# Attention, a routed MLP and a gated MLP in one kernel: eight ScalarE products issued later in each tile, and the weight ring placed 64 bytes off

## The chip, the cores and the metric

The kernel runs on one core of one Trainium2 chip, as one program. The metric is the device time of that program in microseconds (us). Before the change it is 657.42 us, the median of three runs (657.04 to 659.06).

## The reference, cut to what matters

```python
# 1. recurrent attention, B=4, H=8, S=768, D=48
for t in range(S):
    cur = u * kt (outer) vt
    y[t] = rt . (state + cur)
    state = w * state + kt (outer) vt
# 2. a routed MLP on x = y as (3072, 384): 8 experts, 384 -> 1024 -> 384
do_compute = x @ w_skip > 0
e = argmax(x @ w_gate); g = softmax at e
out = x + g * relu(x @ w1[e]) @ w2[e]    # only where do_compute
# 3. a gated MLP
out = (((x @ w1) * (x @ w2)) @ w3) @ w_out
```

The term with `u` (each token's own key and value, the bonus) needs no state: for each token and head it is one number, z = sum over d of r*u*k, times the vector v.

## The kernel before, in words

**Attention (0 to about 178 us).** The 3072 tokens are cut into 24 tiles of 128 (two batches of 64 tokens each), and a loop over n = 0 to 21 is software-pipelined by hand; two last tiles follow it, written out. Each engine runs its instructions in the order in which the loop emits them. In iteration n:

- VectorE makes FK of tile n+2 (`prep`, L359, two SBUF tensors multiplied), scales the state S (`state_copy`, L407, in two iterations of four), evacuates the masked scores Fs of tile n+1 (`evac`, L371), reduces z of tile n+1 (`bonus`, L389), and later adds the bonus to the result of tile n: xg (`x_out`, L440).
- TensorE makes the scores sc of tile n+1 (L366), the result y of tile n (`y_mm`, L419 and L422) in one of two PSUM banks, called y and G in turn, the router's logits of tile n-1 (L464, into a corner of the same bank), three transposes T of tile n-1 (`x_trans`, L451), and the new state (`ds_mm`, L435). Between them `keep` puts matmuls of W = w3 @ w_out (L711, bank wp), a product that the third part needs, or filling matmuls (L255) where its inputs are not there.
- ScalarE copies the state to SBUF (Ss, L409), takes a step of narrowing the 64-bit weights (L103), makes the bonus products zv of tile n+1 (`prep_v`, L399: one ACTIVATE for each of 8 heads, v times z), copies the turned x out of bank T (xT, L453), the logits L (L467) and, where a block of W is done, its high half W_hi (L683). VectorE takes the low half W_lo behind it (L691).
- GpSimd multiplies m (L384, L385: the r*u*k that z sums) and kd (L378).

Tiles are routed in groups of 6, 6, 4, 4 and 4. When a group is full, `route_a` (VectorE) finds the expert of each token, and `route_b` in the next iteration counts by matmul (L507, L509, L510, into a corner of bank G or y); ScalarE copies the counts out (r_pr, L516). The next logits go into the same bank as the counts, and wait for that copy. `run_todo`, called in the middle and at the end of an iteration, issues the steps that are due. The middle of an iteration before the change:

```python
w_step(WN[n][0])
prep_v(n + 1)
w_ready()
y_mm(n)
keep(4 * WK[n][0])
run_todo()
if n > 0:
    x_trans(n - 1)
keep(4 * WK[n][1])
w_step(WN[n][1])
w_evac(0)
x_out(n)
ds_mm(n)
```

**Experts (about 200 to 347 us).** Each of 64 weight pieces (raw, from DRAM, buffers `stg`) is split by ScalarE into ehi (L84) and by VectorE into elo (L85) in a ring of ten pairs: three in pool `ring0`, allocated from the upper end of SBUF beside `stg0`, seven in `ring1`. TensorE reads ehi and elo as stationary operand in L929 and as moving operand in L948. All of this is fp32 in two parts.

**Gated MLP (to the end).** Six blocks of 512 tokens: matmuls L1129 and L1149.

SBUF pools are stacked, so a tile's address follows from the sizes of those before it. Before the change the ring, and everything stacked above or below it, begins at a multiple of 128 bytes.

Of the kernel before, what the change touches and what calls it, by code (L numbers as in the profile page):

```python
# [8 lines left out]
F32 = mybir.dt.float32  # L9
# [9 lines left out]
P = 128  # L19
# [38 lines left out]
def fused_kernel(ctx, tc, att, kv, wt, u, wg, we, w3, wo, w12, r, k, v, wu, out):  # L58
# [18 lines left out]
    E(tc.tile_pool(name="edge", bufs=1, side="right")).tile([P, 24], F32, name="edge")  # L77
    stg = [E(tc.tile_pool(name="stg0", bufs=2, side="right")), None]
    rctx = ExitStack()
    rings = [rctx.enter_context(tc.tile_pool(name="ring0", bufs=RG, side="right")), None]  # L80
    yctx = ExitStack()

# [110 lines left out]
    def load_expert(e, q):  # L193
        raw = stg[(4 * e + q) % 3 // 2].tile([P, 2, 2 * D], F32, name="raw")
        nc.sync.dma_start(out=raw, in_=we[e, :, 2 * q:2 * q + 2, :])
        return raw
# [29 lines left out]
    with tc.manual_schedule():  # L226
# [10 lines left out]
        def load_t(n):  # L237
            nc.sync.dma_start(out=TB[n % 3].rearrange("p a h t -> p (a h t)"), in_=att[n])
# [51 lines left out]
        for i in range(6):  # L290
            wn = pw[:, i - 1] if i else wc
            n = 1 << i
# [62 lines left out]
        def prep(n):  # L355

            t = TB[n % 3]
            FK = FK_[n] = wk.tile([P, 2, NH, CH], F32, name="FK", bufs=3)
            nc.vector.tensor_tensor(out=FK, in0=t, in1=UT[:, n // 2 % 2], op=ALU.mult)  # L359

        def scores(n):
            FK = FK_[n]
            sc = ps_1.tile([P, 512], F32, tag="sc", name="sc").rearrange("p (h t) -> p h t", h=NH)
            for h in range(NH):
                for m, d in zip(half, dims):
                    nc.tensor.matmul(sc[m, h], FK[d, 1, h], FK[d, 0, h], start=True, stop=True)  # L366
            return sc

        def evac(n, sc):
            Fs = Fs_[n] = wk.tile([P, NH, CH], F32, name="Fs")  # L370
            nc.vector.tensor_tensor(out=Fs, in0=sc, in1=mask[:, None, :].to_broadcast([P, NH, CH]), op=ALU.mult)  # L371

        def prep_k(n):

            c, bp = divmod(n, 2)
            if c < NC - 1:
                kd = kd_[n] = wk.tile([P, NH, HD], F32, name="kd")
                nc.gpsimd.tensor_tensor(out=kd, in0=KV[bp][c % 2][:, 1], in1=KU[:, c % 2], op=ALU.mult)  # L378

        def prep_m(n):  # L380

            c, bp = divmod(n, 2)
            m = P_[n] = wk.tile([P, NH, HD], F32, name="m")
            nc.gpsimd.tensor_tensor(out=m, in0=KV[bp][c % 2][:, 0], in1=un, op=ALU.mult)  # L384
            nc.gpsimd.tensor_tensor(out=m, in0=KV[bp][c % 2][:, 1], in1=m, op=ALU.mult)  # L385

        def bonus(n):
            z = z_[n] = wk.tile([P, 32], F32, name="z")[:, 0:NH]
            nc.vector.tensor_reduce(out=z, in_=P_.pop(n), axis=AX.X, op=ALU.add)  # L389

        def prep_v(n, eng=None):
            c, bp = divmod(n, 2)
            v, z = KV[bp][c % 2][:, 2], z_.pop(n)
            zv = zv_[n] = wk.tile([P, NH, HD], F32, name="zv")
            if eng:
                eng.tensor_tensor(out=zv, in0=v, in1=z[:, :, None].to_broadcast([P, NH, HD]), op=ALU.mult)
            else:
                for h in range(NH):
                    nc.scalar.activation(out=zv[:, h], in_=v[:, h], func=AF.Copy, scale=z[:, h:h + 1])  # L399

        def state_copy(n):
            c, bp = divmod(n, 2)
            s = S[bp]
            if c == 0:
                return
            if c % 2 == 0:
                nc.vector.tensor_tensor(out=s, in0=s, in1=w128[:, :, None].to_broadcast([P, NH, HD]),  # L407
                                        op=ALU.mult)
            nc.scalar.copy(out=Ss[bp], in_=s)  # L409

        def y_mm(n, tag="y"):

            c, bp = divmod(n, 2)
            v, Fs, FK = KV[bp][c % 2][:, 2], Fs_.pop(n), FK_.pop(n)
            y = G if n % 2 and n < NT - 2 else ps_1.tile([P, 512], F32, tag=tag, name="y")
            yv = y[:, 0:D].rearrange("p (h d) -> p h d", h=NH)
            for h in range(NH):
                for m in half:
                    nc.tensor.matmul(yv[m, h], Fs[m, h], v[m, h], start=(h == 0), stop=True, skip_group_check=True)  # L419
            for h in range(NH if c else 0):  # L420
                for m, d in zip(half, dims):
                    nc.tensor.matmul(yv[m, h], FK[d, 0, h], Ss[bp][d, h], start=False, stop=True,  # L422
                                     skip_group_check=True)
            y_[n] = y
            if n < NT - 2:
                yb[0] = y
# [19 lines left out]
        def x_trans(n, bank=None):  # L446
            xg = x_.pop(n)
            xb_[n] = T if bank is None else bank
            pT = xb_[n][:, 0:D].rearrange("p (k t) -> p k t", k=ND)
            for k in range(ND):  # L450
                nc.tensor.transpose(pT[:, k], xg[:, P * k:P * k + P], ident)  # L451
            xT_[n] = wk.tile([P, ND, P], F32, name="xT", bufs=2)
            nc.scalar.copy(out=xT_[n], in_=pT)  # L453
# [137 lines left out]
        def place_mm(bp=0):  # L591
            for o, oh, v in pend:
                nc.tensor.matmul(SL[bp][:, o], oh, v, start=False, stop=True, skip_group_check=True)
            pend.clear()
# [78 lines left out]
        def w_step(k):  # L673
            for _ in range(k):
                next(wprep, None)
# [3 lines left out]
        def w_evac(k):  # L679

            while k < len(w_out):
                f, ps = w_out[k]
                nc.scalar.copy(out=W_hi[:, f], in_=ps)  # L683
                w_out[k:k + 1] = []
                w_lo.append((f, ps))
# [8 lines left out]
        def w_ready():  # L694
            done.update(fresh[0])
            fresh[:] = [fresh[1], []]
# [22 lines left out]
        def idle_mm():  # L719
            if spare[0] is None and (w_out or w_lo):  # L720
                w_evac(0)
                w_evac2()
            dummy(DQ)
            dummy(DQ)

        def keep(k):

            due[0] += k
            while due[0] > 0:
                if next(wmm, None):  # L730
                    due[0] -= 4
                else:
                    idle_mm()
                    due[0] -= 2
# [28 lines left out]
        def run_todo(late=False):  # L763
            now, todo[:] = todo[:], []
            for fn, args in now:
                if late and fn is route_b:
                    todo.append((fn, args))
                    continue
                fn(*args)
                if fn is logits_out:  # L770
                    if args[0] in last_of:
                        todo.append((route_a, (last_of[args[0]],)))
                elif fn in NEXT:
                    todo.append((NEXT[fn], args))

        for n in range(NT - 2):
            w_ready()
            if n == NT - 3:
                raws = {q: load_expert(0, q) for q in range(2)}
            if n + 4 < NT:  # L780
                load_t(n + 4)
            prep(n + 2)
            state_copy(n + 1)
            sc = scores(n + 1)
            prep_k(n + 1)
            prep_m(n + 2)
            evac(n + 1, sc)
            bonus(n + 1)
            if n == NT - 3:
                bonus(NT - 1)  # L790
            next(more_consts, None)
            w_step(WN[n][0])
            prep_v(n + 1)
            w_ready()
            y_mm(n)
            keep(4 * WK[n][0])
            run_todo()
            if n > 0:
                x_trans(n - 1)
            keep(4 * WK[n][1])  # L800
            w_step(WN[n][1])
            w_evac(0)
            x_out(n)
            ds_mm(n)
            place_mm(n % 2)
            if n + 4 < NT:
                load_v(n + 4)
            if n < NT - 3:
                place(3)
            w_step(WN[n][2])  # L810
            run_todo(n < NT - 3)
            if n > 0:
                todo.append((logits, (n - 1,)))
            w_evac2()
# [41 lines left out]
    M = mctx.enter_context  # L856
# [40 lines left out]
        w_evac2()  # L897
    wctx.close()
    stg[1] = M(tc.tile_pool(name="stg1", bufs=1, reuse_waits="tile"))
    rings[1] = M(tc.tile_pool(name="ring1", bufs=NRING - RG, reuse_waits="tile"))  # L900
    nr2 = M(tc.tile_pool(name="nr2", bufs=1, reuse_waits="tile"))

# [463 lines left out]
```

## Time and profile before

| | us |
|---|---|
| median of 3 runs | 657.42 |
| the profiled execution | 658.01 |
| its span, first to last instruction | 656.2 |
| TensorE matmul busy | 625.2 (95%) |
| VectorE busy | 364.1 (55%) |
| ScalarE busy | 255.5 (39%) |
| GpSimd busy | 140.3 (21%) |
| mean granted TensorE clock | 0.984 |

Busy shares are over the whole span. The three parts have different limits, so the engine that matters is read stage by stage: which wait ends last there. In the timeline a row is start, duration, engine, line, operation, output<-inputs, shapes and count; brackets give the engine's idle time before it and what ended it.

### The profile page before, as it was taken

The numbers are of one execution on the slowest core, as the hardware profiler recorded it, in microseconds if no ns is written. First come the engines' busy times: TensorE is split into PE (matmuls) and PEld (weight loads), VectorE is DVE, ScalarE is ACT, GpSimd is POOL, SyncE is SP. The second block draws the span as 40 slices with busy tenths as digits, with TensorE's granted clock in tenths as the row PEclk, the third lists the DMA queues.
The fourth block names the chain that finished last, engine by engine and source line by source line (L and its number), as shares of the span: only waits on it lengthen the run. The fifth ranks groups of instructions, "written<-read, shape, count | busy, mean of one in ns | idle before, by whom it ended". The sixth has DMA issues, their size and how long they took to land.

```text
span 656.2 us, 14005 instructions
## 1 busy us (share of the span) xinstructions
PE 625.2 (95%) x5866; PEld 537.9 (82%) x5866; DVE 364.1 (55%) x641; ACT 255.5 (39%) x592; POOL 140.3 (21%) x134
## 2 busy tenths in 40 slices
PE   7979599997998999999999999999999999999996
PEld 6868487886767999999997888888888888888884
DVE  6699897997567889899874321321330330331320
ACT  2556454343325556666643222222221231221220
POOL 4887365543122123223122000000000000000000
PEclk9899899997999999999999999999999999999998
DMA  8889778554427878877522002002002002001001
GB/s 312 339 284 374 257 263 292 191 161 131 137 79 261 269 253 258 297 283 259 186 68 67 0 17 80 1 17 80 1 16 81 1 16 81 0 1 49 0 2 52
DMA packets 26791, 90.53 MB, mean 138 GB/s; under 512 B 4009, under 2 KB 10298, under 8 KB 25696
## 3 DMA queue, kind: packets, MB, share of 16 engines
q1 hardware_dynamic: 24672, 84.11, 37.1%
q0 software_dynamic: 2048, 5.44, 2.3%
q8 instruction: 48, 0.79, 0.5%
q14 instruction: 23, 0.19, 0.1%
HBM read 77.81 MB, written 12.58 MB: 138 GB/s over the span
## 4 chain that ended last, share of the span: by engine, by line
PE 76%; DVE 9%; issue 5%; DMA 4%; ACT 2%; POOL 1%; SPq 0%; ACTq 0%; DVEq 0%; POOLq 0%
PE ab L1129 30%; PE po L1149 15%; PE hp L929 8%; PE y L948 8%; PE wp L711 4%; DMA TB<-in_att 2%; PE sc L366 2%; DVE FK L359 1%; PE S L435 1%; ACT zv L399 1%; PE G L464 1%; DMA KV<-in_kv 1%; PE y L422 1%; PE y L419 1%; PE pT L1109 1%
## 5 line engine op out<-in xcount | busy, mean ns | idle before, releaser
L1136 DVE TENSOR_TENSOR p_sb<-ab,a_sb 128x512 f32<-128x512 f32 x48 | 33.2, 692 | 155.6 <-PE ab L1129 155.6
L1129 PE MATMUL ab<-bxh,w12h 128*128 128x512 f32 x288 | 112.4, 390 | 0.6 <-ACT bxh L1168 0.6
L1129 PE MATMUL ab<-bxh,w12l 128*128 128x512 f32 x288 | 112.1, 389 | 0.0
L1129 PE MATMUL ab<-bxl,w12h 128*128 128x512 f32 x288 | 112.0, 390 | 0.0
L1137 ACT CAST ph<-p_sb 128x512 fp32r<-128x512 f32 x48 | 29.8, 622 | 106.4 <-DVE p_sb L1136 106.4
L85 DVE TENSOR_TENSOR elo<-raw,ehi 128x768 fp32r<-128x768 f32 x64 | 60.8, 956 | 8.7 <-ACT ehi L84 8.3
L1129 PEld LDWEIGHTS ab<-bxh,w12h 128*128 128x128 f32 x288 | 54.1, 188 | 12.6 <-ACT bxh L1168 1.5
L1129 PEld LDWEIGHTS ab<-bxl,w12h 128*128 128x128 f32 x288 | 54.0, 188 | 11.7 <-DVE bxl L1170 0.4
L1129 PEld LDWEIGHTS ab<-bxh,w12l 128*128 128x128 f32 x288 | 54.1, 188 | 11.2
L399 ACT ACTIVATE zv<-KV,z 128x48 f32<-128x48 f32 x184 | 44.0, 324 | 34.1 <-issue 17.8
L1149 PE MATMUL po<-ph,W_hi 128*128 128x512 f32 x144 | 57.0, 396 | 0.0
L1149 PE MATMUL po<-pl,W_hi 128*128 128x512 f32 x144 | 56.1, 390 | 0.0
L929 PE MATMUL hp<-xh,ehi 128*128 128x256 f32 x192 | 54.9, 287 | 1.3 <-ACT xh L880 0.9
L1149 PE MATMUL po<-ph,W_lo 128*128 128x512 f32 x144 | 56.0, 389 | 0.0
L711 PE MATMUL wp<-wo_s,w 128*128 128x384 f32 x128 | 52.8, 525 | 3.3 <-DVE w L118 2.2
L84 ACT CAST ehi<-raw 128x768 fp32r<-128x768 f32 x64 | 52.7, 829 | 2.9 <-DMA raw<-in_we 2.9
L929 PE MATMUL hp<-xh,elo 128*128 128x256 f32 x192 | 53.8, 282 | 0.0
L929 PE MATMUL hp<-xl,ehi 128*128 128x256 f32 x192 | 53.7, 282 | 0.0
L1138 DVE TENSOR_TENSOR pl<-p_sb,ph 128x512 fp32r<-128x512 f32 x48 | 33.3, 693 | 33.0 <-ACT ph L1137 33.0
L932 ACT ACTIVATE hh<-hp 128x256 fp32r<-128x256 f32 x64 | 24.7, 386 | 49.4 <-PE hp L929 47.6
L948 PE MATMUL y<-ehi,hh 128*128 128x384 f32 x128 | 43.3, 338 | 0.0
L948 PE MATMUL y<-elo,hh 128*128 128x384 f32 x128 | 43.2, 338 | 0.0
(207 smaller groups left out, 1174.7 us busy)
## 6 DMA issues: line engine op xcount, KB each, us to landing
raw<-in_we SPq DMA_DIRECT2D x32, 768.0 KB, 5.6
KV<-in_kv SPq DMA_DIRECT2D x24, 576.0 KB, 5.1
TB<-in_att SPq DMA_DIRECT2D x24, 512.0 KB, 8.0
raww<-in_w SPq DMA_DIRECT2D x8, 1024.0 KB, 8.5
raw<-in_w SPq DMA_DIRECT2D x8, 768.0 KB, 7.4
xm<-xg SPq DMA_DIRECT2D x48, 96.0 KB, 2.2
out<-ob SPq DMA_DIRECT2D x18, 256.0 KB, 2.0
x<-xm SPq DMA_DIRECT2D x20, 192.0 KB, 2.5
```

Of the source, the lines that this page charges most:

```text
L84: nc.scalar.copy(out=hi, in_=raw)
L85: (eng or nc.vector).tensor_tensor(out=lo, in0=raw, in1=hi.bitcast(F32), op=ALU.subtract)
L399: nc.scalar.activation(out=zv[:, h], in_=v[:, h], func=AF.Copy, scale=z[:, h:h + 1])
L711: nc.tensor.matmul(ps, w3[:, g], wo_s[:, g], start=(g == 0), stop=(g == NF - 1))
L929: nc.tensor.matmul(hp, a, b, start=(i == 0), stop=(i == 8))
L932: nc.scalar.activation(out=hh, in_=hp, func=AF.Relu)
L948: nc.tensor.matmul(ys[e, t], a[:, P * t:P * t + P], b[:, D:2 * D], start=(f == 0 and i == 0), stop=(f == NF - 1 and i == 2))
L1129: nc.tensor.matmul(q, a, b, start=(i == 0), stop=(i == 8))
L1136: nc.vector.tensor_tensor(out=p_sb, in0=ps[1], in1=a_sb, op=ALU.mult)
L1137: nc.scalar.copy(out=ph, in_=p_sb)
L1138: nc.vector.tensor_tensor(out=pl, in0=p_sb, in1=ph.bitcast(F32), op=ALU.subtract)
L1149: nc.tensor.matmul(po, a[:, f, c], b, start=(i == 0), stop=(i == 3 * NF - 1))
```

## The change

`prep_v(n + 1)` is emitted later in the iteration: behind the first `run_todo()` (which issues the counts' copy) and behind `x_trans(n - 1)` (which issues the copy of turned x). It is still ahead of `w_evac(0)`, `x_out(n)` and the second `run_todo` with the logits' copy. Two unused tiles of 64 bytes are allocated, one between `stg0` and `ring0`, one between `stg1` and `ring1`. So the ring, and what is stacked beyond it (the buffers of the narrowed weights, the gathered tokens xr, raw2), begin 64 bytes past a multiple of 128; `stg` (raw) stays at a multiple of 128.

```diff
     stg = [E(tc.tile_pool(name="stg0", bufs=2, side="right")), None]
     rctx = ExitStack()
+    rctx.enter_context(tc.tile_pool(name="edge0", bufs=1, side="right")).tile([P, 16], F32, name="edge0")
     rings = [rctx.enter_context(tc.tile_pool(name="ring0", bufs=RG, side="right")), None]
...
             w_step(WN[n][0])
-            prep_v(n + 1)
             w_ready()
             y_mm(n)
             keep(4 * WK[n][0])
             run_todo()
             if n > 0:
                 x_trans(n - 1)
+            prep_v(n + 1)
             keep(4 * WK[n][1])
...
     stg[1] = M(tc.tile_pool(name="stg1", bufs=1, reuse_waits="tile"))
+    M(tc.tile_pool(name="edge1", bufs=1, reuse_waits="tile")).tile([P, 16], F32, name="edge1")
     rings[1] = M(tc.tile_pool(name="ring1", bufs=NRING - RG, reuse_waits="tile"))
```

No engine gets or loses an instruction, and the orders of TensorE, VectorE, GpSimd and the DMA queues stay as they were. Only ScalarE's order changes. Around the counts of the first group, before (zv is the product of `prep_v`, W_hi<-wp the copy of a block of W, r_d the router's exponential, r_pr the counts):

```order
L399 ACTIVATE zv<-KV_0_110,z 128x48 x8
L683 CAST W_hi<-wp_118 128x384
L494 ACTIVATE r_d_1243<-r_d_1243 128x48
L453 COPY xT<-T 128x384
L103 ACTIVATE w_1287<-raww 128x1024
L467 COPY L<-y 128x9
L409 COPY Ss_112<-S_191 128x384
L399 ACTIVATE zv<-KV_1_109,z 128x48 x8
L516 COPY r_pr<-G 128x48
L453 COPY xT<-T 128x384
L467 COPY L<-G 128x9
```

and ScalarE at the same place in the changed kernel, whose lines stand one lower:

```order
L684 CAST W_hi<-wp_122 128x384
L495 ACTIVATE r_d_1238<-r_d_1238 128x48
L454 COPY xT<-T 128x384
L400 ACTIVATE zv<-KV_0_114,z 128x48 x8
L104 ACTIVATE w_1291<-raww 128x1024
L468 COPY L<-y 128x9
L410 COPY Ss_116<-S_195 128x384
L517 COPY r_pr<-G 128x48
L454 COPY xT<-T 128x384
L400 ACTIVATE zv<-KV_1_113,z 128x48 x8
L468 COPY L<-G 128x9
```

W_hi and r_d now stand ahead of one zv, and r_pr ahead of the next; w, L and Ss stand behind the first. One block of W later, on ScalarE, around the counts of the second group, before:

```order
L399 ACTIVATE zv<-KV_1_111,z 128x48 x8
L494 ACTIVATE r_d_1959<-r_d_1959 128x48
L453 COPY xT<-T 128x384
L683 CAST W_hi<-wp_118 128x384
L103 ACTIVATE w_2002<-raww 128x1024
L467 COPY L<-y 128x9
L409 COPY Ss_112<-S_191 128x384
L399 ACTIVATE zv<-KV_0_108,z 128x48 x8
L516 COPY r_pr<-G 128x48
```

and ScalarE there in the changed kernel:

```order
L495 ACTIVATE r_d_1954<-r_d_1954 128x48
L454 COPY xT<-T 128x384
L400 ACTIVATE zv<-KV_1_115,z 128x48 x8
L684 CAST W_hi<-wp_122 128x384
L104 ACTIVATE w_2006<-raww 128x1024
L468 COPY L<-y 128x9
L410 COPY Ss_116<-S_195 128x384
L517 COPY r_pr<-G 128x48
```

Here zv moves between xT and W_hi: W_hi, with VectorE's W_lo waiting for it, keeps its place behind zv, but zv now stands behind the transposes' copy. The third counts (16 tiles in) combine both: r_pr moves ahead of zv, and the W_hi that follows stays behind it.

## Rows read from the trace of the kernel before

**Rows 1.** The page, part 2: TensorE's busy tenths in 40 slices of 16.4 us.

```profile
PE   7979599997998999999999999999999999999996
```

**Rows 2.** Waits of TensorE, 0 to 200 us: total us, times, longest.

```profile
PE G L464 <- ACT r_pr L516: 10.2, 3, 6.0
```

**Rows 3.** Timeline, 66 to 84 us: counts of the first group.

```profile
69.62 0.56 DVE L691 TENSOR_TENSOR W_lo<-wp,W_hi 128x384 fp32r<-128x384 f32 x1 [0.90 <-ACT W_hi L683]
...
70.80 0.24 ACT L494 ACTIVATE r_d<-r_d 128x48 f32<-128x48 f32 x1 [1.22 <-DVE r_oh L493]
...
72.41 0.49 ACT L409 COPY Ss<-S 128x384 f32<-128x384 f32 x1
...
76.23 1.91 ACT L399 ACTIVATE zv<-KV,z 128x48 f32<-128x48 f32 x8 [3.33 <-issue]
...
78.04 0.18 ACT L516 COPY r_pr<-G 128x48 f32<-128x48 f32 x1
...
78.27 1.45 PE L464 MATMUL G<-wgs,xT 128*128 128x9 f32 x6 [5.96 <-ACT r_pr L516]
...
83.46 1.11 PE L366 MATMUL sc<-FK 48*64 48x64 f32 x32
```

**Rows 4.** Timeline of TensorE, 20 to 50 us: an earlier stall.

```profile
39.07 0.91 PE L711 MATMUL wp<-wo_s,w 128*128 128x384 f32 x2 [2.18 <-DVE w L118]
```

**Rows 5.** Windows: busy us of PE, PEld, DVE, ACT, POOL; clock; DMA share, GB/s.

```profile
78.20:82.70 4.50, 4.43 (x13) 2.99 (x13) 2.75 (x9) 0.57 (x3) 0.00 (x0) 0.53 0.21 56
```

**Rows 6.** Waits of VectorE, 79 to 111 us.

```profile
DVE xg L440 <- PE G L464: 2.0, 1, 2.0
DVE xg L440 <- ACT zv L399: 1.5, 1, 1.5
DVE xg L440 <- PE y L464: 1.4, 2, 0.8
DVE Fs L371 <- PE sc L366: 1.0, 1, 1.0
```

**Rows 7.** Timeline, 117 to 127 us: a block of W, counts of the second group.

```profile
117.32 0.48 ACT L453 COPY xT<-T 128x384 f32<-128x384 f32 x1 [0.70 <-PE T L451]
...
118.21 0.56 DVE L691 TENSOR_TENSOR W_lo<-wp,W_hi 128x384 fp32r<-128x384 f32 x1
...
123.65 0.84 PE L464 MATMUL G<-wgs,xT 128*128 128x9 f32 x6 [0.47 <-ACT r_pr L516]
...
124.58 0.56 DVE L440 TENSOR_TENSOR xg<-G,zv 128x384 f32<-128x384 f32 x1 [0.82 <-issue]
...
124.96 0.48 ACT L453 COPY xT<-T 128x384 f32<-128x384 f32 x1 [1.36 <-PE T L451]
...
126.84 1.11 PE L366 MATMUL sc<-FK 48*64 48x64 f32 x32
```

**Rows 8.** Timeline, 152 to 162 us: counts of the third group.

```profile
152.33 0.48 ACT L409 COPY Ss<-S 128x384 f32<-128x384 f32 x1 [2.00 <-DVE S L407]
...
155.40 1.45 PE L464 MATMUL G<-wgs,xT 128*128 128x9 f32 x6 [3.74 <-ACT r_pr L516]
...
159.42 0.56 DVE L691 TENSOR_TENSOR W_lo<-wp,W_hi 128x384 fp32r<-128x384 f32 x1
...
161.19 1.11 PE L366 MATMUL sc<-FK 48*64 48x64 f32 x32
```

**Rows 9.** Waits of VectorE, 153 to 178 us.

```profile
DVE xg L440 <- PE G L464: 4.8, 2, 3.2
...
DVE xg L440 <- PE y L464: 2.1, 1, 2.1
```

**Rows 10.** Windows by stage, columns as in rows 5.

```profile
118.00:153.00 35.00, 33.20 (x722) 27.28 (x720) 33.49 (x55) 13.64 (x51) 17.60 (x15) 1.00 0.51 160
```

**Rows 11.** Line L359, FK: ns min/median/max, first and last start.

```profile
L359 DVE TENSOR_TENSOR FK<-TB,UT x24: 1204/1219/2024, 6.2 to 167.7; 128x1024 f32<-128x1024 f32 x24
```

**Rows 12.** Line L399, zv: ns min/median/max, first and last start.

```profile
L399 ACT ACTIVATE zv<-KV,z x184: 317/321/348, 12.6 to 171.9; 128x48 f32<-128x48 f32 x184
```

## The prediction

> **What bounds the kernel now.** I read the page's slices first, because a change in one stage is worth only what that stage waits for. TensorE is at nine tenths or more in all slices of the gated MLP but the last and in most of the expert stage; the thinnest slice from the start on is the fifth, 66 to 82 us, at five tenths, and the tenth, 148 to 164 us, falls to seven [rows 1]. Both lie in the attention loop. So whatever the loop gains, the two MLPs behind it begin that much earlier and are otherwise as long as before. Next I asked which wait of TensorE in the loop is the longest: the logits wait for ScalarE's copy of the counts, 10.2 us in three times, 6.0 at most [rows 2]. The timeline shows why. At the first group's counts, ScalarE copies Ss at 72.41, and its next instructions are the eight products zv, which wait for VectorE's z: zv begins at 76.23. The counts' copy, one instruction of 0.18 us whose input lay ready, stands behind them and begins at 78.04; TensorE has idled 5.96 us by then [rows 3]. And it pays twice: from 78.2 to 82.7 its granted clock is 0.53, the lower of its two levels (1.2 of 2.4 GHz) [rows 5], so that the way from these logits to the next scores takes 83.46 - 78.27 = 5.19 us [rows 3], where it takes 126.84 - 123.65 = 3.19 us after the second group's counts [rows 7], which cost a wait of only 0.47. The third group's counts repeat the first: 3.74 us idle, then 161.19 - 155.40 = 5.79 us to the scores [rows 8].
>
> **The change, part by part.** Nothing is added or removed but two unused tiles; zv moves behind r_pr and xT on ScalarE, and no DMA or instruction of another engine moves past anything. zv itself is needed only by the xg of the following iteration, behind a whole round of TensorE's work, so its delay has cover; if that went, the price is at most its own 1.91 us an iteration.
>
> *First counts.* W_hi now stands ahead of zv; its block of W was done, and VectorE's W_lo waited 0.90 us for it [rows 3]. VectorE is that much earlier in all that follows, and so is r_d, from 70.80 to 69.90. From r_d to Ss takes 72.41 - 70.80 = 1.61 us; one zv now lies between, 1.91; Ss takes 0.49: r_pr can begin at 73.91 instead of 78.04. TensorE follows 0.23 later (78.27 - 78.04), at 74.14: 4.13 us earlier. Its idle time is then 5.96 - 4.13 = 1.83 us. An idle time of 2.18 us [rows 4] was followed by two matmuls in 0.91 us, as fast as anywhere in the loop, so I take the full clock and 3.19 us for the way to the scores: they begin at 77.33 instead of 83.46. **TensorE gains 6.13 us.** VectorE gains 0.90 and the 2.0 that xg waited for these logits, 2.9 us; up to 111 us it then waited another 1.5 + 1.4 + 1.0 = 3.9 us for TensorE (the wait put down to zv ended with logits of the same moment) [rows 6]. With TensorE 6.13 ahead these waits shrink until VectorE has caught up: it needs 3.2 of the 3.9.
>
> *Second counts.* Here the change costs. xT waits for TensorE, so it comes at 117.32 - 6.13 = 111.19; W_lo came 118.21 - 117.32 = 0.89 behind it, and zv now lies between xT and W_hi: W_lo begins at 111.19 + 0.89 + 1.91 = 113.99, a gain of 4.22 and no longer 6.13. VectorE's queue stands behind W_lo: the next FK, Fs and z. From 118 to 153 us VectorE is busy 33.5 of 35 us [rows 10], so it sets the pace and the 1.91 us are lost. The 0.82 that xg waited behind the counts [rows 7] should close, since TensorE is ahead: 5.04 us.
>
> *Third counts.* In the trace's own times, r_pr can begin when Ss ends, 152.33 + 0.48 = 152.81, and the logits 0.23 later at 153.04, 2.36 earlier; the scores after 3.19 at 156.23 instead of 161.19. **TensorE gains another 4.96 us.** The W_hi behind zv: xT comes 124.96 - 123.65 = 1.31 after logits at full clock, 154.35; W_lo 0.89 + 1.91 later, 157.15 instead of 159.42 [rows 7, 8]. So VectorE gains only 2.27 there, but it then waits for TensorE again, 2.1 and 4.8 - 3.2 = 1.6 us [rows 9], and these cover the missing 2.7.
>
> *Two other blocks of W* in the loop (W_hi near 96 and 143 us) also keep their place behind zv. At the first VectorE lags TensorE, at the second zv waits for z in both orders: nothing.
>
> *The ring.* No row shows ehi or elo 64 bytes off. The nearest is zv: every second of its 48-column slices reads and writes 64 bytes past a multiple of 128, and all 184 lie between 317 and 348 ns with a median of 321 [rows 12]; the half that is off cannot be dearer or cheaper than the other by more than about the 4 ns between minimum and median, 1.2%. On the 147 us of the expert stage (200 to 347) that is 1.8 us either way. I take 0, since the row shows no two groups. VectorE's and ScalarE's splits lie beside full TensorE there and would have to grow by more than that to be seen.
>
> *The sum.* 5.04 + 4.96 = 10.0 us off the profiled execution's 658.01, 648.0 us. The median of the runs, 657.42, lies 0.6 lower, so the forecast is **647.4 us**. Its own range: 1.9 more if W_lo finds VectorE late and the second place costs nothing, 1.8 either way for the ring, and 2.4 less gained (next rival): 644 to 651.5.
>
> **A row against it, and a rule.** VectorE's FK takes 1.20 us at least and 2.02 at most, median 1.22 [rows 11], one thing that the sum takes as fixed: the long ones overlap GpSimd's multiplies. The Trainium skill has a rule for this ("SBUF — State Buffer", Who interferes with whom): a VectorE instruction with two SBUF inputs and a GpSimd one that reads SBUF exclude each other, and the one issued later blocks. By that rule a shift of VectorE against GpSimd, which follows TensorE's state matmuls, makes new pairs; the sum would be about 650.
>
> **Rivals.**
> 1. *New collisions* of VectorE with GpSimd. Before 111 us they cost little (VectorE has 0.7 of its waits to spare, and at the second counts 1.9 more). From 118 to 153, where VectorE sets the pace, three FK that now take 1.22 us could take 2.02: 3 x 0.8 = 2.4 us, 649.8; with Fs and the narrowing steps hit likewise, twice that, 652.2. For it: the spread of rows 11. Against: the shift can also free those that collide now.
> 2. *The wait only changes its name.* If TensorE finds after r_pr that VectorE's scores or xT are not there, the lead is not kept. VectorE's own waits alone remain as the gain: 0.9 + 2.0 + 3.2, less W_lo's 1.9 and 0.9 = 3.3 us, 654.1. If even these close, no change, 657. Against: it is VectorE that waits for TensorE at these places now, not the reverse [rows 6, 9].
> 3. *Slower: W_hi behind zv.* VectorE takes W_lo in order, and behind it stand FK and Fs, which TensorE and then zv wait for. Were VectorE ahead of ScalarE at each of the three blocks whose W_hi now follows an xT and a zv ready to run (near 96, 118 and 159 us), it costs 3 x 1.91 = 5.7 us. It decides from the point where r_pr gives less than that, that is if ScalarE, with w, L and Ss behind zv, reaches r_pr no earlier than now: 657.4 + 5.7 - 0.9 = 662.2. Against: r_pr has 4.1 us of room at the first counts and 2.4 at the third.
> 4. *The ring is dearer for TensorE* by the 1.8 us, with no gain in the loop: 659.2. That the ring does nothing is what I expect; that it gives 1.8 belongs to my range.
>
> **How the numbers follow.** The forecast has 0.64, the collisions 0.14, the lead that is not kept 0.08, no change 0.08, W_hi 0.04, the ring 0.02. A measurement of this kernel can tell about 0.3%, 2.0 us, from no change: faster 0.64 + 0.14 + 0.08 = 0.86, same 0.08, slower 0.06. The range that holds 8 in 10 takes the forecast's own range, the bounds of the ring and the collisions, up to where VectorE's waits alone are gained: 644 to 654.
>
> **What would show it right or wrong.** Right: TensorE's logits wait for r_pr about 1.8 us at the first counts and 1.3 at the third, and the clock there stays near 1.00; the stage up to the experts is 10 us shorter, and the MLPs as long as before. W_lo waits for W_hi near 112 us, by about 1.9, and again, by about 0.9, at the third counts. The matmuls on ehi and elo keep their mean durations within 1.2%. Wrong: a new wait of TensorE for Fs or FK as long as the old one; W_lo waits at three places; FK near 2.0 us between 110 and 145; or a gain or a loss in the expert stage, which would be the ring's.

## The result, and the profile after

The changed kernel takes 652.58 us (median of 4 runs, 652.17 to 652.92), the kernel before in the same comparison 658.24 (4 runs, 657.04 to 659.63): 0.9913 of it, 95% interval 0.9889 to 0.9937. That is 5.7 us less, where 10.0 were forecast. The profiled execution took 652.92 us with a span of 651.2, against 656.2. The first expert matmul starts at 195.61 us instead of 200.49, so 4.9 of the span's 5.0 us come from the attention loop, as forecast; the two MLPs are as long as before.

The page's line of TensorE and its waits up to 200 us, which answer to [rows 1, 2]:

```profile
PE   7989899998989999999999999999999999999996
```

```profile
PE G L465 <- ACT r_pr L517: 4.7, 3, 2.1
```

The fifth slice has risen from five tenths to eight, and the wait for the counts' copy from 10.2 us in three times to 4.7. The same place in the timeline as [rows 3] (start, duration, engine, line, what, in brackets the idle time before it):

```profile
73.91 0.47 ACT L410 COPY Ss<-S 128x384 f32<-128x384 f32 x1
74.28 0.20 ACT L517 COPY r_pr<-G 128x48 f32<-128x48 f32 x1
...
74.53 1.31 PE L465 MATMUL G<-wgs,xT 128*128 128x9 f32 x6 [2.13 <-ACT r_pr L517]
75.69 0.88 PE L452 MATMUL T<-ident,xg 128*128 128x128 f32 x3
76.37 2.77 PE L712 MATMUL wp<-wo_s,w 128*128 128x384 f32 x4
79.06 1.52 PE L436 MATMUL S<-KV,kd 64*48 64x48 f32 x32
80.38 1.65 PE L367 MATMUL sc<-FK 48*64 48x64 f32 x32
```

r_pr came at 74.28, 0.37 later than forecast. But from the logits to the scores it took 80.38 - 74.53 = 5.85 us, not 3.19: the four products for W, 2.77 us here, take 1.46 behind the second group's logits. TensorE gained 3.08 us at these scores (83.46 before), not 6.13. Of the difference, 2.66 us is that slow way and 0.37 the later r_pr: this execution came late to the counts (it began the scores ahead of them at 68.36 us, the one before the change at 67.39). The windows behind the two long waits, and the stretch of [rows 10]:

```profile
74.50:79.00 4.50, 4.47 (x13) 2.85 (x13) 4.43 (x12) 2.33 (x10) 0.58 (x1) 0.52 0.77 265
...
150.00:155.00 5.00, 4.98 (x21) 3.29 (x23) 3.08 (x18) 2.70 (x11) 0.00 (x0) 0.50 0.79 265
```

```profile
118.00:153.00 35.00, 32.40 (x613) 26.53 (x608) 33.67 (x64) 13.02 (x52) 15.13 (x13) 0.95 0.53 173
```

The granted clock is 0.52 and 0.50 behind idle times of 2.13 and 2.08 us: the lower of the two levels (1.2 of 2.4 GHz), as before the change behind 5.96 and 3.74. VectorE is busy 33.67 of the 35 us, as before. The second and the third group's counts, as in [rows 7, 8]:

```profile
116.38 0.56 DVE L692 TENSOR_TENSOR W_lo<-wp,W_hi 128x384 fp32r<-128x384 f32 x1 [1.06 <-ACT W_hi L684]
...
119.78 0.84 PE L465 MATMUL G<-wgs,xT 128*128 128x9 f32 x6 [0.52 <-ACT r_pr L517]
```

```profile
149.40 0.48 ACT L410 COPY Ss<-S 128x384 f32<-128x384 f32 x1 [0.98 <-DVE S L408]
149.78 0.19 ACT L517 COPY r_pr<-G 128x32 f32<-128x32 f32 x1
...
150.02 1.45 PE L465 MATMUL G<-wgs,xT 128*128 128x9 f32 x6 [2.08 <-ACT r_pr L517]
...
156.01 1.40 PE L367 MATMUL sc<-FK 48*64 48x64 f32 x32
```

W_lo near 116 us is 1.83 us earlier than before and has the new wait for W_hi; 4.22 were forecast. Yet the second group's scores are 126.84 - 122.97 = 3.87 us earlier. The copies of the state (Ss) and of the counts ahead of them, before the change and then behind it:

```profile
120.47 0.48 ACT L409 COPY Ss<-S 128x384 f32<-128x384 f32 x1 [1.18 <-DVE S L407]
...
123.42 0.18 ACT L516 COPY r_pr<-G 128x48 f32<-128x48 f32 x1
```

```profile
119.14 0.48 ACT L410 COPY Ss<-S 128x384 f32<-128x384 f32 x1 [1.69 <-DVE S L408]
119.52 0.20 ACT L517 COPY r_pr<-G 128x48 f32<-128x48 f32 x1
```

Here too r_pr stood behind zv before: it came 2.95 us after Ss began, and now comes 0.38 after it. The third group's scores are 161.19 - 156.01 = 5.18 us earlier, again behind a slow way of 5.99 us.

Two things stayed open. Was the missing part the clock, and would TensorE's lead be worth anything to VectorE if the clock held? And does the ring do nothing?

### The profile page after: what moved, and what is told of

Read it like the earlier page. It is cut to its first block, busy times and chain, and to the rows that moved or that the text cites. A ratio compares the mean times of both kernels' runs of the same rounds, so it can differ in the third digit from the quotient of the medians.

```text
span 651.2 us, 14007 instructions
## 1 busy us (share of the span) xinstructions
PE 627.9 (96%) x5866; PEld 540.1 (83%) x5866; DVE 364.6 (56%) x641; ACT 253.5 (39%) x592; POOL 141.3 (22%) x134
## 4 chain that ended last, share of the span: by engine, by line
PE 66%; DVE 13%; DMA 10%; issue 6%; ACT 2%; POOL 1%; SPq 0%; DVEq 0%; POOLq 0%; ACTq 0%
PE ab L1131 30%; PE po L1151 15%; PE hp L931 4%; PE y L950 4%; PE wp L712 4%; DMA TB<-in_att 3%; DMA xm<-yo,sidx 3%; DMA xr<-xm,sidx 3%; DVE FK L360 2%; PE sc L367 1%; PE S L436 1%; DVE w L119 1%; DVE elo L86 1%; DVE Fs L372 1%; PE G L465 1%
## 5 line engine op out<-in xcount | busy, mean ns | idle before, releaser
L950 PE MATMUL y<-ehi,hh 128*128 128x384 f32 x128 | 43.4, 339 | 0.0
L950 PE MATMUL y<-ehi,hl 128*128 128x384 f32 x128 | 43.2, 337 | 0.0
```

Of the source, the lines that this page charges most:

```text
L950: nc.tensor.matmul(ys[e, t], a[:, P * t:P * t + P], b[:, D:2 * D], start=(f == 0 and i == 0), stop=(f == NF - 1 and i == 2))
```

## The experiments

Every diff but the second is against the changed kernel. Each ratio is to the kernel before in runs of the same comparison, with its 95% interval.

**The move alone**, the two unused tiles left out:

```diff
-    rctx.enter_context(tc.tile_pool(name="edge0", ...
-    M(tc.tile_pool(name="edge1", ...
```

> zv moved behind r_pr and xT, the ring where it was before (no edge tiles). Theory (the move does all of it): the same as the change, 0.991 of the kernel before, 652.6 us within 1; the expert stage as long as in both. Rival (the ring's 64 bytes gave 1.8 of the 5.7 us): 654.4 us, and the expert matmuls hp at 282 to 283 ns median instead of 279. Rival (the ring costs and hides a larger gain): 650.8 us.

Measured: 652.37 us, 0.9907 (0.9874 to 0.9939). The move does all of it.

**The ring alone**, against the kernel before:

```diff
+    rctx.enter_context(tc.tile_pool(name="edge0", ...
+    M(tc.tile_pool(name="edge1", ...
```

> The edge tiles alone, zv where it was before. Theory: no difference, 1.000 within 0.002 (658 us). Rival: 1.8 us less, 656.4 (0.997), or 1.8 us more, 660 (1.003), and then in the stretch from the first expert matmuls to the end, while the way to them stays 200 us.

Measured: 658.03 us, 0.9984 (0.9954 to 1.0015): no difference that can be told. In the changed kernel the expert matmuls on elo had a mean of 279 ns where they had 282 before, which looked like the ring; one line each, of the changed kernel and of the ring alone (line and operation, count, busy us, mean ns):

```profile
L931 PE MATMUL hp<-xh,elo 128*128 128x256 f32 x192 | 53.3, 279 | 0.0
```

```profile
L931 PE MATMUL hp<-xh,elo 128*128 128x256 f32 x192 | 53.9, 283 | 0.0
```

With the same ring the mean is 283, so the 3 ns (0.6 us on the 192 of a kind) are not the ring's. From the first expert matmul to the end it takes 455.5 us in this run's profile, 455.7 in the kernel before, and 455.2 to 456.2 in all fourteen profiles of this document: what sets these runs apart lies ahead of the experts.

**W_hi ahead of zv:**

```diff
                 x_trans(n - 1)
+            w_evac(0)
             prep_v(n + 1)
```

> The change, with the block's W_hi copied ahead of zv at every place. Theory (W_hi behind zv costs VectorE something only where VectorE sets the pace): the waits of W_lo for W_hi (1.08, 1.06 and 0.90 us in the changed kernel) go; the one near 116 us is gained, perhaps part of the one near 96, the one near 155 is covered by VectorE's waits for TensorE behind it: 1.0 to 2.0 us less, 651.1 (0.9893). Rival (VectorE finds TensorE or ScalarE late behind W_lo): the waits get another name, 652.6 (0.9913). Rival (W_hi's 0.46 us ahead of zv delays zv and with it xg): 653 to 654.

Measured: 652.59 us, 0.9915 (0.9884 to 0.9947): no gain over the change. VectorE's waits for W_hi fell from 3.4 us in four times (60 to 180 us) to 1.5 in three, none over 0.5. The time is the second theory's, the wait got another name: TensorE waited 2.87 us for r_pr at the second group, and the clock was 0.50 there (120.3 to 126.3 us). That W_hi's place brought this wait is not shown, since the change itself has it in another execution (below). So the forecast's price for W_hi behind zv was real as a wait, but its removal gives nothing back in the median.

**The clock held by products of zeros:**

```diff
                 fn(*args)
+                if fn is route_b and args[0] in (0, 2):
+                    for _ in range(26):
+                        nc.tensor.matmul(T[:, D:D + P], zb[:, 0:P], zb[:, 0:P], start=True, stop=True)
```

> The change, with 26 products of zeros (128 columns each, into columns of the bank T that nothing uses) between the counts and the logits of the first and the third group; it adds work and moves none. Theory (what was missing of the forecast is the clock's fall behind the idle 2.1 us): the granted clock stays near 1.00 from 74.5 to 82 and from 150 to 157 us, and the way from logits to scores takes 3.2 us instead of 5.9. VectorE then has 0.5 us of waits for TensorE and 2.1 for W_hi to give up until 118 us and about 8 behind 153, so 0.5 to 2.6 us are gained at the first place and 2.6 at the third: 647.4 to 649.5, 648.5 (0.985). Rival (the clock falls anyway, whatever fills the gap): 652.6 or, if the products reach beyond r_pr, up to 1 us more. Rival (the clock stays but VectorE sets the pace at both places): 652.6 with a clock of 1.00.

Measured: 652.66 us, 0.9915 (0.9884 to 0.9946): the median gains nothing and misses the theory's 648.5, though the profiled run, with 650.36 us the shortest of its six, has the clock that the theory said at both places. Its windows as above, and TensorE at the first, the second and the third group:

```profile
74.50:79.00 4.50, 4.50 (x91) 3.69 (x93) 4.50 (x10) 3.21 (x12) 1.56 (x2) 1.00 0.83 294
...
150.00:155.00 5.00, 5.00 (x113) 4.19 (x111) 3.27 (x14) 2.71 (x11) 1.57 (x2) 1.00 0.52 156
```

```profile
72.76 1.61 PE L773 MATMUL T<-zb 128*128 128x128 bf16 x26
74.49 0.84 PE L465 MATMUL G<-wgs,xT 128*128 128x9 f32 x6
...
77.68 1.11 PE L367 MATMUL sc<-FK 48*64 48x64 f32 x32
...
119.20 0.84 PE L465 MATMUL G<-wgs,xT 128*128 128x9 f32 x6 [2.41 <-ACT r_pr L517]
119.89 0.53 PE L452 MATMUL T<-ident,xg 128*128 128x128 f32 x3
120.25 1.83 PE L712 MATMUL wp<-wo_s,w 128*128 128x384 f32 x4
122.01 1.52 PE L436 MATMUL S<-KV,kd 64*48 64x48 f32 x32
123.33 1.69 PE L367 MATMUL sc<-FK 48*64 48x64 f32 x32
...
153.17 1.11 PE L367 MATMUL sc<-FK 48*64 48x64 f32 x32
```

With the gap filled the clock is 1.00 and the way to the scores is 77.68 - 74.49 = 3.19 us, the forecast's number. The scores are 5.78 us earlier than before the change. At the second group only 126.84 - 123.33 = 3.51 of it are left: r_pr is late there (2.41 us, in the change 0.52), and the clock falls at that place instead. At the last scores ahead of the third group's counts it is 147.70 - 144.77 = 2.93, and behind them 161.19 - 153.17 = 8.02 us, 5.09 more. What holds r_pr at the second group is VectorE's S: Ss, ahead of r_pr on ScalarE, waits 1.49 us for it, and VectorE has been full since the first group. The stretch from 84 to 118 us, of the change and of this run:

```profile
84.00:118.00 34.00, 34.00 (x719) 28.17 (x720) 29.75 (x42) 17.55 (x60) 20.38 (x16) 1.00 0.81 275
```

```profile
84.00:118.00 34.00, 32.24 (x709) 26.82 (x704) 33.83 (x45) 17.15 (x59) 20.62 (x15) 1.00 0.74 260
```

VectorE is busy 33.83 of 34 us instead of 29.75, and now TensorE is the one that has gaps. Part of that is the same instructions taking longer. VectorE's routing steps of the first group and GpSimd's product kd, in the change and then in this run:

```profile
78.51 0.20 DVE L471 TENSOR_TENSOR r_q<-r_pr,r_ohb 128x48 f32<-128x48 f32 x1
...
80.57 1.22 DVE L360 TENSOR_TENSOR FK<-TB,UT 128x1024 f32<-128x1024 f32 x1
...
80.68 1.97 POOL L379 TENSOR_TENSOR kd<-KV,KU 128x384 f32<-128x384 f32 x1 [5.60 <-PE S L436]
```

```profile
77.94 1.45 POOL L379 TENSOR_TENSOR kd<-KV,KU 128x384 f32<-128x384 f32 x1 [2.94 <-PE S L436]
...
78.43 1.02 DVE L471 TENSOR_TENSOR r_q<-r_pr,r_ohb 128x48 f32<-128x48 f32 x1
...
82.58 1.22 DVE L360 TENSOR_TENSOR FK<-TB,UT 128x1024 f32<-128x1024 f32 x1
```

kd follows TensorE's S, so a faster TensorE brings it forward, onto the routing steps. r_q takes 1.02 us instead of 0.20 and ends at 79.45, just behind kd (77.94 + 1.45 = 79.39); from r_q to FK it takes 4.15 us instead of 2.06. All of that is in three steps, each of which ends 0.03 to 0.07 us behind a product of GpSimd: r_q, r_hf (0.65 instead of 0.17) and the first r_o (1.02 instead of 0.21). So TensorE's 2.7 us bring VectorE 2.0 us of loss. The Trainium skill's rule ("SBUF — State Buffer", Who interferes with whom), by which a VectorE instruction with two SBUF inputs and a GpSimd one that reads SBUF exclude each other, agrees with r_q and kd.

**zv one tile later:**

```diff
             if n > 0:
+                prep_v(n)
                 x_trans(n - 1)
-            prep_v(n + 1)
...
```

> zv of tile n instead of n + 1 between r_pr and xT: the products are made one tile later, just ahead of their use, so that at the counts neither zv of that iteration nor xT stands ahead of w, L, Ss and r_pr, and W_hi follows xT directly. Theory: at the first counts r_pr begins when Ss ends, about 72.9 instead of 74.3 us, TensorE idles 0.7 instead of 2.13 and keeps a clock of 1.00; W_lo waits for W_hi nowhere by over 0.5; at the second and third counts Ss waits for VectorE's S, so r_pr gains nothing there. VectorE has 0.5 us of waits for TensorE and 2.1 for W_hi to give up until 118: 1 to 2.6 us less than the change, 650.5 (0.988). Rival (VectorE is full from the first counts on, and GpSimd's products fall on its short routing steps): TensorE's lead ends as a wait of 2.4 us or more for r_pr at the second counts, 652.6 (0.9915). Rival (xg now waits for zv): 654 or more.

Measured: 656.28 us, 0.9978 (0.9954 to 1.0003), most of the change's gain lost. The rival in which xg waits for zv held; VectorE's waits from 60 to 200 us of that run (total, times, longest):

```profile
DVE xg L441 <- ACT zv L400: 8.5, 7, 2.3
```

The forecast said that zv's delay has a whole round of cover. It does, and this run shows what it is worth: without it, seven waits of VectorE.

**The routing steps ahead of xg**, with the products of zeros:

```diff
...
+                elif fn is route_b:
+                    route_c(*args)
+                    hold.append(1)
...
-                place(3)
+                place_mm() if hold else place(3)
+                hold.clear()
```

> The run with the zero products, and VectorE's twelve routing steps behind the counts' copy (r_q to val) moved ahead of xg and the narrowing step w; nothing else. In the run with the zero products GpSimd began kd at 77.9 instead of 80.7 us and VectorE's chain from r_q to FK took 78.43 to 82.58, 4.15 us, instead of 78.51 to 80.57, 2.06. Theory (the order decides what GpSimd's products hit): the chain begins near 76.8 and half of it is through before kd, FK begins 0.5 to 1.5 us earlier, the wait for r_pr at the second counts falls from 2.4 to 1.0 to 1.9: 1 us less than with the zero products alone, 650 to 651.5 (0.988). Rival (VectorE and GpSimd share whatever stands there, so the long steps xg and w are hit instead): FK at 82.6 as before, the same time, 651.5 to 652.6.

Measured: 649.5 us, 0.9879 (0.9838 to 0.9920). By its ratio the time is the theory's (0.988), by the microseconds it lies just below 650 to 651.5; but the profile can't carry it: TensorE stood still for 1.9 us ahead of 67.66 us in that execution, for no cause that the profile shows, kd came before the routing steps, and these took 2.15 us untouched. The two runs with the filled gap below settle it.

**The gap filled with work that is due anyway:** where counts stand, the turning of x and the products for W go ahead of the logits; the routing steps as in the run before.

```diff
...
+            if todo and todo[0][0] is route_b:
+                held = todo[1:]
+                del todo[1:]
+                run_todo()
+                x_trans(n - 1)
+                keep(4 * WK[n][1])
+                todo += held
+                run_todo()
+                prep_v(n + 1)
+            else:
...
```

> The change, with work of the same iteration in the gap instead of zero products: where counts stand, the turning of x and the products for W go ahead of the logits (and the routing steps ahead of xg, as in the run before). Theory: the gap of 2.1 us is filled with 1.9 us of work that had to be done anyway, so TensorE is another 1.9 us earlier at the first and the third group than with zero products, with a clock of 1.00; at the first VectorE sets the pace and nothing more is gained, at the third, where VectorE waits for TensorE about 8 us, 1 to 1.9 are: 649.5 (0.9865). Rival (xT and with it xg come no earlier, since VectorE is full): the same as with the zero products, 651 to 652.6. Rival (logits later, and xg with them): 653 to 654.

Measured: 648.46 us, 0.9867 (0.9822 to 0.9911), where the theory said 0.9865.

**A third of GpSimd's products left out**, with the products of zeros:

```diff
-            nc.gpsimd.tensor_tensor(out=m, in0=KV[bp][c % 2][:, 1], in1=m, op=ALU.mult)
...
```

> The run with the zero products, with GpSimd's third product of a tile (m by k) left out in all 24 tiles, so that the bonus is computed without k: a third of GpSimd's work less from 15 us on. Theory (VectorE, lengthened by GpSimd's products, is what keeps TensorE's lead from being gained): VectorE's FK, w and routing steps above their shortest time add up to 27 us over the loop's second half; a third of that, 9 us, goes, and the time falls by 4 to 9 us, 643.5 to 648.5 (0.981). Rival (VectorE is late for another reason, its own steps or ScalarE's copies): less than 2 us.

Measured: 647.0 us, 0.9844 (0.9800 to 0.9888): 0.0071 less than with the zero products alone, 4.7 us of 658. The two were measured on different chips, so this goes by the ratios, whose intervals meet at 0.9884 to 0.9888. The time lies in the theory's range, though not all of it lies in the second half: VectorE's twelfth FK already comes at 69.14 us instead of 72.11. The stretch from 84 to 118 us again:

```profile
84.00:118.00 34.00, 33.71 (x719) 28.18 (x714) 29.02 (x49) 17.29 (x59) 14.41 (x10) 1.00 0.79 273
```

Against the run with the zero products GpSimd's busy time fell by 6.2 us and VectorE's by 4.8, though VectorE lost no instruction: the five FK in this stretch take 6.08 us instead of 7.99, so GpSimd had lengthened them.

The last four ran on one chip, the change among them.

**zv between r_pr and xT:**

```diff
             run_todo()
+            prep_v(n + 1)
             if n > 0:
                 x_trans(n - 1)
-            prep_v(n + 1)
```

> The change, but zv between r_pr and xT: it no longer stands ahead of the counts' copy, as in the change, but still ahead of the turned x, as before it. Theory (the counts' place does all of it; xT has over 2 us of room, since ScalarE waits 2.2 us for its turning): as the change, 0.9913 (652.6); xT comes up to 0.6 us later at the first counts, W_lo waits for W_hi up to 1 us less, both covered. Rival (zv waits for z and holds xT, and the logits of the next iteration wait for xT): 654 to 656. Rival (the waits for W_hi, 2.1 us until 118, are gained): 650.5.

Measured: 651.88 us, 0.9886 (0.9872 to 0.9900), as the change beside it. So it is the counts' copy whose place matters; that of the turned x makes no difference that these runs can tell.

**The filled gap alone**, VectorE's order as in the change:

> The change, with the turning of x and the products for W ahead of the logits where counts stand, and VectorE's order as in the change (the routing steps behind xg). Theory (the filled gap is what gains, the routing steps' place does nothing, since GpSimd's products fell on them at either place): as the run with both, 0.987 (648.5), with a lead of 3.3 us of TensorE behind the first counts that shrinks to under 1 by the second, and 5 us gained at the third. Rival (the routing steps ahead of xg give half of it): 650.5 to 651.5.

Measured: 647.09 us, 0.9835 (0.9803 to 0.9867). TensorE at the third group:

```profile
147.65 0.18 PE L511 MATMUL G<-acc,ones 128*128 128x32 bf16 x1
147.67 0.53 PE L452 MATMUL T<-ident,xg 128*128 128x128 f32 x3
148.03 1.46 PE L712 MATMUL wp<-wo_s,w 128*128 128x384 f32 x4
149.32 0.73 PE L465 MATMUL G<-wgs,xT 128*128 128x9 f32 x6
149.99 0.92 PE L436 MATMUL S<-KV,kd 64*48 64x48 f32 x32
150.74 1.11 PE L367 MATMUL sc<-FK 48*64 48x64 f32 x32
```

There is no gap and no slow instruction; the scores come 156.01 - 150.74 = 5.27 us before the change's. At the first scores TensorE was 80.38 - 76.84 = 3.54 us ahead of the change, at the second group's it still had 122.97 - 121.61 = 1.36 us, where the theory said under 1, and at the scores next to 144 us 0.1 of it was left. The time lies a little below the theory's 648.5 and clear of the rival's 650.5 to 651.5: the routing steps' place gives nothing that shows.

**The filled gap with the routing steps, again:**

> The run with the filled gap and the routing steps ahead of xg once more, beside the change on the same chip. Theory: 0.987 of the kernel before, 4 us less than the change, and of that next to nothing before 147 us and 5 us at the third counts. Rival (its first comparison was lucky by 2 us): 0.990, 1 to 2 us less than the change.

Measured: 649.04 us, 0.9853 (0.9838 to 0.9869), nearer to the theory's 0.987 than to the rival's 0.990.

**The change again:**

> The change itself once more, for the comparison of the others on this chip. Theory: 0.991 within 0.002, a clock near 0.5 behind the idle 2.1 us at the first and the third counts. Rival (the clock's fall is a matter of chance, as behind the narrowing step near 39 us): 1.00 at one of the two places, and 2.7 us less there.

Measured: 652.33 us, 0.9897 (0.9883 to 0.9911). The time is as expected, the profile answers to neither theory: that execution, at 656.24 us the longest of its five, came to the first counts 5.5 us late, again with an idle time of 1.9 us without a cause in the profile, ahead of 62.64 us. Its three logits:

```profile
80.07 0.84 PE L465 MATMUL G<-wgs,xT 128*128 128x9 f32 x6 [0.29 <-ACT r_pr L517]
...
125.15 1.03 PE L465 MATMUL G<-wgs,xT 128*128 128x9 f32 x4 [2.87 <-ACT r_pr L517]
...
156.52 0.84 PE L465 MATMUL G<-wgs,xT 128*128 128x9 f32 x6 [0.28 <-ACT r_pr L517]
```

Here only the second group had a long wait, and the clock was 0.75 from 122 to 128 us and 1.00 behind the other two (80 to 85 and 153 to 160 us). Which group pays thus differs between executions of one kernel. Three unfilled runs, with W_hi ahead of zv, with zv between r_pr and xT, and this one, came to the scores ahead of the first counts 1.8 to 7.1 us later than the change's first profile (70.12, 71.26 and 75.50 us against 68.36); all three waited 0.29 us at the first counts and 2.87 at the second.

Beside this run the two filled gaps are 5.2 and 3.3 us shorter (medians), and their intervals lie below the change's. **The filled gap beats both kernels**; whether the routing steps are moved makes no difference that these runs can tell.

## Why the prediction was right in direction and too large

*Right.* The time came from where it was looked for: the counts' copy behind zv. The median, 652.58 us, lies above the forecast's own range (644 to 651.5) and within the one that holds 8 in 10 (to 654); what made it late, the clock, is in no rival, so that it lies within the wider range is partly luck. VectorE gained 2.9 us at xg, as forecast (76.91 instead of 79.81). The MLPs kept their length, and the ring did nothing; the two rivals that end slower did not come. W_hi behind zv cost what was said at the third counts (a wait of 0.90 us), 1.06 instead of 1.9 near 116 us, and 1.08 near 95 us, where nothing was forecast.

*The step that failed first* is "so I take the full clock and 3.19 us for the way to the scores". It was taken from one row, the stall of 2.18 us that kept the clock [rows 4]. In the changed kernel the same stall of the same length was followed by a clock of 0.65 (39.4 to 43.4 us), and both waits for r_pr by 0.52 and 0.50. The term was 5.85 and 5.99 us instead of 3.19 twice: 2.7 us too little at the first counts, 2.8 at the third. With the gap filled by zeros the same terms came out at 3.19 and 153.17 - 150.03 = 3.14, and TensorE's two gains at 5.78 and 5.09 where 6.13 and 4.96 were forecast.

*The step that failed second* is "these waits shrink until VectorE has caught up: it needs 3.2 of the 3.9", with W_lo at 113.99. The waits did shrink: from xg at the first counts to W_lo near 116 us VectorE waited 4.8 us before the change, and behind it 2.2 besides its waits for W_hi. But of the 2.9 us that it had gained at xg, only 1.83 were left at W_lo (116.38) where 4.22 were forecast. Two things took the rest: W_hi, with 1.08 + 1.06 us of waits instead of one of 1.9, and FK, two of which are long in the change and had taken 1.22 us each before (97.00 and 103.30):

```profile
95.65 2.04 DVE L360 TENSOR_TENSOR FK<-TB,UT 128x1024 f32<-128x1024 f32 x1
...
101.87 2.02 DVE L360 TENSOR_TENSOR FK<-TB,UT 128x1024 f32<-128x1024 f32 x1
```

Ahead of each a product of GpSimd had just begun (95.61 and 101.72 us); before the change kd began behind FK at both places (97.19 and 104.27), and FK kept its 1.22. The gain at xg and the waits that went, less those for W_hi and less FK, are 2.9 + 2.6 - 2.14 - 1.62 = 1.7 us. The run with the zero products shows the same more sharply: TensorE was 5.8 us ahead, the profile lists no wait of VectorE on this way, and yet W_lo came only 2.22 us earlier than before the change:

```profile
115.99 0.56 DVE L692 TENSOR_TENSOR W_lo<-wp,W_hi 128x384 fp32r<-128x384 f32 x1
```

The sum held VectorE's own durations fixed. They are not: when its waits go, GpSimd's products, which had run while it waited, fall on its instructions. That is the forecast's first rival, but it was looked for on FK behind 118 us and said to cost little before 111; it came before, in the change on these two FK, in the run with the zero products on two FK as well (102.64 and 108.33 us) and on the short routing steps near 80 us (2.1 us).

*A term that was too small.* At the second counts the sum had 0.82 us besides VectorE's gain. But r_pr stood behind zv there too, as at the other two, and moved 2.57 us nearer to Ss (2.95 to 0.38). So the second scores came 3.87 us earlier although W_lo gave only 1.83. In the run of the move alone, whose loop is the same, r_pr was 0.54 us earlier at the first counts than forecast, and these scores came 126.84 - 121.82 = 5.02 us earlier, against 5.04 forecast: that the number was met there is luck, with one term too large and one too small.

*The sum.* Of the 10.0 us, 4.9 came. At the last scores ahead of the third counts TensorE had 147.70 - 143.98 = 3.72 us where 5.04 was forecast; the third counts gave 5.18 - 3.72 = 1.46 where 4.96 was. The second shortfall, 3.5 us, is the larger: 2.8 of it is the clock (5.99 against 3.19), 0.7 the wait at these counts (2.08 against 3.74 - 2.36 = 1.38). The first, 1.3 us, is hardly more than two executions differ by: the run of the move alone came to its first counts' copy at 73.37 us instead of 74.28, kept about that lead, and had 147.70 - 142.85 = 4.85 us at the same scores and 161.19 - 154.91 = 6.28 behind the third counts. There nearly all of the shortfall is at the third counts, 1.43 of 4.96. The filled gap shows it from the other side: it has 3.84 us at the last scores ahead of the third counts and 161.19 - 150.74 = 10.45 at those behind them. That its median, 647.09 us, is near the forecast's 647.4 says little for the forecast, which was for another kernel and reached its number by other terms.

What stays open: why the zero products, whose profiled execution has 8.0 us at the third scores, gain nothing in the median over the change. Only one of its six executions was profiled, and it was the shortest. How much of VectorE's fuller time, in the run with the zero products, is GpSimd's doing and how much is work that only moved forward was shown for one place (2.1 us) and, by leaving products out, for the whole (4.7 us of the time), not for each instruction.

## What to carry to other kernels

Where an in-order queue makes TensorE wait, look first at every place where the moved instruction stood ahead of the awaited one: here there were three, and the sum priced two of them in full. Then look at what remains of the wait after the move, not only at what is taken from it: a rest of 2 us cost another 2.7 here at the lower clock, and independent work put into the gap gave both back. One row that kept its clock is no rule; price the way behind a gap at both levels. And when a lead is handed to an engine that is nearly full, let its durations grow: what ran beside its waits will run beside its work.

## What the runs showed that was not expected

*The idle time's length does not tell what the clock does behind it.* Behind 2.18 us the clock stayed at 1.00 in the kernel before (39.0 to 43.0 us) and fell to 0.65 in the changed one. Behind 1.28 us it fell in the run with zv between r_pr and xT (third group), and behind 1.39 us it stayed in the filled gap's second run (second group, 118 to 126 us at 1.00):

```profile
152.40:157.40 5.00, 4.93 (x25) 3.25 (x27) 4.18 (x19) 2.84 (x12) 0.00 (x0) 0.53 0.72 251
```

```profile
118.00:126.00 8.00, 6.06 (x143) 5.47 (x142) 7.72 (x21) 2.88 (x11) 4.21 (x4) 1.00 0.42 145
```

In the run with the zero products the two steps right behind 2.41 us of idle time still ran at full speed (0.84 and 0.53 us) and the next three did not. No run here tells what decides it.

*A short instruction of VectorE can cost as much as a long one.* Beside a GpSimd product of 128x384 elements a step on 128x48 took 1.02 us instead of 0.20, and of eleven such steps three were hit. That a chain of small steps is a worse place for GpSimd's work than a long step is not shown: moving the chain ahead of xg made no difference that the runs can tell.
